# A's small softmax in smaller pieces, and the first stacked loads two per slot, in a kernel of two attentions

## The chip, the core and the metric

The kernel runs on one core of a Trainium2 chip. The metric is the device time of one execution in microseconds, as the median of several runs. A core has a matrix engine (PE, whose weight loads are shown apart as PEld), a vector engine (DVE), a scalar engine (ACT), a general engine (POOL) and a queue that starts DMAs (SP); ACT and POOL can start DMAs too. Each engine takes its instructions strictly in the order in which the program wrote them, and an instruction that waits holds up all behind it on its engine.

## What is computed

Two attentions over 2048 positions with 32 heads of 18 columns, each with its own input, its own projection and its own output matrix; the results stand side by side. A looks, from each position, at eight positions: itself and seven earlier ones, two apart. B looks at all positions.

```python
S, D, H, Dh, W, dil = 2048, 576, 32, 18, 8, 2
# A: q, k, v = heads of x @ wqkv
idx = arange(S)[:, None] - arange(W)[None, :] * dil      # masked where negative
logits = einsum("bhsd,bhswd->bhsw", q, k[idx]) * Dh ** -0.5
a = einsum("bhsw,bhswd->bhsd", softmax(logits), v[idx]) @ wo
# B: q, k, v = heads of x @ wqkv
scores = einsum("bhqd,bhkd->bhqk", q, k) * Dh ** -0.5
b = einsum("bhqk,bhkd->bhqd", softmax(scores), v) @ wo
out = concatenate([a, b], axis=-1)
```

## The kernel before

**Projections (up to about 415 us).** Inputs and weights are split into a high and a low part (L413, L414), and PE multiplies the parts (L303, L366). The products of B's queries and keys leave PSUM through ACT (L504, L505) and POOL (L506) and are stored by SP (L511) in a DRAM buffer `dqk`, those of A in `da` (L694, L695). The later part of this stage runs in *slots*: `stream` puts one product after the other on PE, and after each calls `slot()`, which takes one list of functions off `todo`. `at(n, f)` puts a function n slots on.

**Stacked queries and keys.** For four heads at a time (a *group* g, eight of them) queries and keys are read back from `dqk` in the layout that PE wants: `stack_loads(g)` returns twelve loads of 288 KB (L142, L143). For g = 0, 1 and 2 POOL issues them, in the slots of the projections. `second_rows` (L620) plans those of g = 1: it runs in a slot, and from there each load gets a slot of its own, from the fifth on.

**Steps.** After that there are 512 steps: eight groups times four *blocks* of 512 queries times sixteen key tiles. The blocks are numbered n = 0 to 31. Each step has four scores on PE (L271), four exponentials on ACT (L279), the product with the values of an earlier step's exponentials (L744), and, for later blocks, pieces of the row maxima: matmuls (L160) into a ring of three PSUM banks, each reduced by DVE (L168). PE can't refill a bank until DVE has reduced it. A block's maxima become a negative row that is loaded into the stacked queries (`place`, L193), so the first score of a block waits for these loads. Most steps open with the first part of a maximum and score behind it; where `ahead` (L1313) is true, the first score goes first. Before, it is true at a block's first step for n < 6 and n >= 24, unless the step is named in `MADE`.

**A beside it.** A's positions are worked on in eight pieces of 256, j = 0 to 7 (`local`, L902), on POOL and DVE while the steps run. `AT[j]` is the step at which j begins, and `plan` puts every part at a fixed step behind it; `due()` runs, at the end of each step, what is planned for it, so a DVE operation of A stands in DVE's queue behind the reductions of that step. `SOON[j]` moves the softmax of some j forward by one step (j = 4, 5, 6) or three (j = 0). The parts, in their order:

- `match` (L923): nine products of queries and keys on POOL, the last followed by L932, which writes the logits `lg`
- `most` (L945): the maximum over the eight logits, on DVE (L943, tile `am`), in two pieces of 32 columns, at steps 32 and 33 of j
- `lower` (L948, POOL), `exponents` (L951, ACT)
- `total` (L954): the sum, on DVE (L943, tile `as`): two pieces of 32 for j = 0, 2, 5, one of 64 for the others
- `inverses` (L957): two reciprocals on DVE (L959)
- `share` (L961): logits times reciprocals, on POOL (L962)
- `weighted` (L964): nine products with the values on POOL (L968 to L971), then `upper`, `rest`, `put` and `get`, which bring the result through DRAM to PE
- `sums_of_a`: the output product of A (L1260), for the most part in `together` (L1242), which takes two steps in one with the 27 matmuls of such a product beside them: a *pair* of steps, called a paired stretch below. `MADE` names the steps at whose end such a product becomes ready.

`match` of j + 1 begins on POOL soon after `weighted` of j.

Of the kernel before, what the change touches and what calls it, by code (L numbers as in the profile page):

```python
# [11 lines left out]
ALU = mybir.AluOpType  # L12
# [17 lines left out]
SUB = AB // 4  # L30
# [14 lines left out]
MADE = ((96, 101, 112, 128), (144, 160, 176, 192), (208, 212, 224, 240), (256, 266, 272, 288),  # L45
        (307, 320, 336, 352), (368, 376, 384, 400), (417, 432, 440, 448), (474, 476, 478, 480))
# [15 lines left out]
def two_attentions(ctx: ExitStack, tc, xa, wa, woa, xb, wb, wob, out):  # L62
# [45 lines left out]
    step = 0  # L108
# [8 lines left out]
    def due():  # L117
        for f in agenda.pop(step, []):
            f()
# [254 lines left out]
    def do_all(fs):  # L374
        for f in fs:
            f()
# [6 lines left out]
    with (tc.tile_pool(name="x", bufs=1, side="right") as xp,  # L383
# [103 lines left out]
        if True:  # L487
# [47 lines left out]
            ahead = deque()  # L535
# [29 lines left out]
            def at(n, *fs):  # L565

                while len(todo) <= n:
                    todo.append([])
                todo[n].extend(fs)
# [24 lines left out]
            def store_values(h, v2):  # L594
                for i, v in enumerate(v2):
                    load(dv[4 * h + 2 * i : 4 * h + 2 * i + 2].rearrange("g p t c -> p g (t c)"),
                         v.rearrange("p g t h d -> p g (t h d)"))
# [22 lines left out]
            def second_rows():  # L620

                store_values(1, v2)
                kept.close()
                stack1 = ctx.enter_context(tc.tile_pool(name="stack1", bufs=1, reuse_waits="tile"))
                make_set(stack1, 1)
                do_all(ones_loads(1))
                zeros = xp.tile([128, 512], F32, name="ohi", bufs=4)
                nc.gpsimd.memset(zeros[:108, : 16 * HALO], 0.0)
                load(rows(da[0], ((HALO + S) * 16, 108), (HALO + S, 16), (1, HALO)), zeros[:108, : 16 * HALO])
                for i, f in enumerate(stack_loads(1, issue=nc.gpsimd.dma_start)):  # L630
                    at(5 + i, f)
                load_v(0)

            wa_room = ExitStack()
# [48 lines left out]
            for k in range(2, 14):  # L683
                n = 46 if k == 2 else 36 + 4 * k
# [34 lines left out]
            for c, b in order:  # L719
                n = min(128, 3 * D - 128 * c)  # L720
                work_list.append(((b % 2, ws[c][0], xas[b][0], slice(0, n), every),
                                  lambda ps, n=n: ps[:n], lambda ps, c=c, b=b, n=n: leave_a(c, b, n, ps)))
# [12 lines left out]
        step = 0  # L735
# [166 lines left out]
    def local(j):  # L902
# [31 lines left out]
                    for w in range(1, W):  # L934
                        nc.gpsimd.memset(lg[:32, w, : DIL * w], MASKED)

        def over_window(op, name, n, parts=2):

            if n == 0:
                st[name] = work.tile([128, SUB], F32, name=name, bufs=1)  # L940
            some = SUB // parts
            cols = slice(some * n, some * n + some)
            nc.vector.tensor_reduce(st[name][:, cols], st["lg"][:, :, cols].rearrange("p w n -> p n w"), axis=AX.X, op=op)  # L943

        def most(n):  # L945
            over_window(ALU.max, "am", n)

        def lower():  # L948
            nc.gpsimd.tensor_sub(st["lg"], st["lg"], ap(st["am"], (0, W), (1, SUB)))
# [2 lines left out]
            nc.scalar.activation(st["lg"], st["lg"], AF.Exp, scale=SCALE)  # L952

        def total(n):  # L954
            over_window(ALU.add, "as", n, len(sums[0]))

        def inverses(n):  # L957
            half = st["as"][:, SUB // 2 * n : SUB // 2 * n + SUB // 2]
# [5 lines left out]
        def weighted(c):  # L964
            if c == 0:
                st["o"] = work.tile([128, DH, SUB], F32, name="ao", bufs=1)
            at = wide()
            nc.gpsimd.tensor_mul(at, ap(st["lg"], (0, 2), (SUB, W), (1, SUB)), window(st["v"], c))  # L968
            nc.gpsimd.tensor_add(at[:, :, :4], at[:, :, :4], at[:, :, 4:])  # L969
            nc.gpsimd.tensor_add(at[:, :, :2], at[:, :, :2], at[:, :, 2:4])  # L970
            nc.gpsimd.tensor_add(st["o"][:, 2 * c : 2 * c + 2], at[:, :, 0], at[:, :, 1])  # L971
# [10 lines left out]
        def put(i):  # L982
            load(rows(dao[j, i, 0, 0], (DH * SUB, 128), (1, DH * SUB)),
                 ap(st["parts"][i].bitcast(F32), (1, DH * SUB)))
# [24 lines left out]
        def sums_of_a(h, n, alone=True):  # L1009
# [7 lines left out]
            if not alone:  # L1017
# [4 lines left out]


        soon = SOON[j]
        sums = ((36, 37) if j in (0, 2, 5) else (36,), (38, 39))
        late = soon % 3
        pieces = [(33, lower), (35, exponents), (39, share), (60 + late, upper), (61 + late, rest), (64 + late, lambda: put(0)), (66 + late, lambda: put(1))]

        pieces[:0] = [(at, lambda f=f, n=n: f(n)) for f, ats in ((most, (32, 33)), (total, sums[0]),
                                                                (inverses, sums[1])) for n, at in enumerate(ats)]  # L1030
        for c in range(DH // 2):
            pieces.append((39 + 5 * c // 2 + late, lambda c=c: weighted(c)))
        pieces = [(at - soon, f) for at, f in pieces]
        pieces += [(5 + 5 * c // 2, lambda c=c: match(c)) for c in range(DH // 2)]

# [60 lines left out]
    sums = {}  # L1096
# [141 lines left out]
    rest = NG * NB * PIECES * 2 - early  # L1238

    total = early + rest  # L1240
# [47 lines left out]
    while step < ALL:  # L1288
        n, kt = divmod(step, NT)
        g, b = divmod(n, NB)  # L1290
        es = [None] * 4

        if inside and inside[0] in for_two and kt and len(ready) == 1 and total - sum(given) >= 8 and step + 4 < ALL:
            new = together(*inside.pop(0)(False))
            assert not leaving
            due()
            step += 1
            weigh(*ready, new[0])
            ready[:] = new[1:]
            due()  # L1300
            step += 1
            continue

        while leaving:
            leaving.pop()()

        whole = total - sum(given) > 1
        parts = (bool(begun) or total - sum(given) > 3) and step not in copied

        ps = bank() if inside and whole else None  # L1310


        ahead = kt == 0 and (n < 6 or n >= 24) and step not in sum(MADE, ())  # L1313
        part = [parts_of_maximum()] if parts and not ahead else []
        for h in (0, 2, 1, 3):

            if inside and h == 3:
                inside.pop(0)()
            es[h] = score(g, b, kt, h, between=(lambda: part.append(parts_of_maximum())) if parts and ahead and h == 0 else None)
            if h == 0 and whole:  # L1320
                maximum(1, ps)()
            if h == 1 and parts:
                part[0]()
            if h == 3 and whole:
                maximum(0)()
        if sum(given) == total and not begun:
            settle()
        for fs in (behind_scores, outside):
            while fs:
                fs.pop(0)()  # L1330

        paired = paired or kt % 2 == 0 and sum(given) == total and not begun
        for _ in range(1 if paired and step < ALL - 2 else len(waiting)):
            if waiting:
                waiting.pop(0)()
        if ready and (kt % 2 == 0 or not paired):
            weigh(ready.pop(0))
        ready.append((g, b, kt, es))
        if paired and kt % 2:
            weigh(*ready)  # L1340
            ready.clear()
        due()

        if len(waiting) > (0 if not paired else 2 if kt % 2 else len(waiting)):
            waiting.pop(0)()
        step += 1
# [24 lines left out]
```

## Time and profile before

| | |
|---|---|
| median of three runs | 1596.72 us (1595.77 to 1596.78) |
| the profiled execution | 1597.76 us, span 1596.0 us |
| mean granted clock of PE in it | 0.999 |
| PE busy | 1583.2 us (99%) |
| DVE busy | 1367.7 us (86%) |
| ACT busy | 1216.6 us (76%) |
| POOL busy | 964.6 us (60%) |

Engine shares are means over the span. In the order of time, a row has its start and its duration in us, the engine, the line, the operation with what it writes and reads, how many equal instructions are merged in it, and in brackets how long the engine had been idle before it and what ended that. In groups of instructions, the numbers behind the bar are the busy time in us, the mean duration of one in ns, and the idle time before them. Windows give the busy time of every engine in a stretch, with the number of instructions in brackets, and then the granted clock, the DMA share and GB/s. A busy PE is not PE at its peak: matmuls on the two halves of the rows overlap, and the rows don't show by how much.

### The profile page before, as it was taken

What the parts mean: (1) busy time and instruction counts of PE and PEld (TensorE: products, weight loads), DVE (VectorE), ACT (ScalarE), POOL (GpSimd) and SP (SyncE); (2) the same over time, 40 slices, a digit from 0 to 9 for tenths busy, and PEclk for the clock granted to TensorE, in tenths of its full rate; (3) what the DMA queues carried; (4) which work ended last, traced back from release to release, by engine and by line L of the source; (5) the groups of instructions that cost most, each with busy time, mean ns of one, the idle gap of its engine ahead of it and who ended that gap; (6) DMA issues with size and microseconds to landing.
All of it is one profiled execution on the core that took longest, in us unless ns stands there. A gap on an engine that the chain in (4) does not pass through costs nothing.

```text
span 1596.0 us, 34951 instructions
## 1 busy us (share of the span) xinstructions
PE 1583.2 (99%) x13276; PEld 969.1 (61%) x13276; DVE 1367.7 (86%) x2294; ACT 1216.6 (76%) x2438; POOL 964.6 (60%) x798
## 2 busy tenths in 40 slices
PE   9999999999999999999999999999999999999998
PEld 7999889999644445444445445445444444545676
DVE  5199899999999999999989999999999999998622
ACT  6423441211599999999999999999999999998655
POOL 2405742211166996896797897797798699791000
PEclk9999999999999999999999999999999999999999
DMA  8937954622312262245326324522721332154311
GB/s 254 232 124 201 255 178 124 164 90 81 74 34 71 64 143 63 70 118 123 74 67 138 90 79 114 123 67 54 148 89 50 90 94 56 51 166 139 129 60 63
DMA packets 188024, 175.65 MB, mean 110 GB/s; under 512 B 119416, under 2 KB 133240, under 8 KB 186128
## 3 DMA queue, kind: packets, MB, share of 16 engines
q1 hardware_dynamic: 182992, 161.88, 37.0%
q0 software_dynamic: 4032, 10.63, 3.2%
q8 instruction: 104, 1.70, 0.5%
q10 hardware_dynamic: 832, 0.92, 0.2%
q14 instruction: 64, 0.52, 0.1%
HBM read 98.77 MB, written 73.47 MB: 108 GB/s over the span
## 4 chain that ended last, share of the span: by engine, by line
PE 92%; DVE 5%; DMA 1%; ACT 1%; POOL 1%; issue 0%; SPq 0%; POOLq 0%; DVEq 0%; ACTq 0%
PE po L744 29%; PE bank L271 18%; PE bank L160 17%; PE bank L366 15%; PE bank L303 5%; PE bank L1260 4%; PE bank L1133 4%; DVE mx L168 4%; POOL xlo L414 1%; ACT e L279 0%; DMA dqk<-olo 0%; DVE am L943 0%; DMA first<-xb 0%; DMA more<-xa 0%; DMA dqk<-ohi 0%
## 5 line engine op out<-in xcount | busy, mean ns | idle before, releaser
L168 DVE TENSOR_REDUCE mx<-bank 128x2 f32<-128x512 f32 x2048 | 1279.7, 684 | 121.6 <-PE bank L160 91.1
L279 ACT ACTIVATE e<-bank 128x512 f32<-128x512 f32 x2048 | 1048.3, 605 | 61.2 <-PE bank L271 55.3
L160 PE MATMUL bank<-ks,qs 54*128 54x512 f32 (+1 forms) x2466 | 789.0, 381 | 4.2 <-DVE mx L168 3.4
L160 PEld LDWEIGHTS bank<-ks,qs 54*128 54x128 f32 x2466 | 404.1, 184 | 390.2 <-DVE mx L168 343.8
L271 PE MATMUL bank<-qs,ks 56*128 56x512 f32 x2048 | 592.2, 425 | 0.1
L744 PE MATMUL po<-e,v 128*19 128x512 f32 x4096 | 531.3, 598 | 0.0
L271 PEld LDWEIGHTS bank<-qs,ks 56*128 56x128 f32 x2048 | 308.3, 184 | 25.5 <-ACT e L279 18.8
L925 POOL TENSOR_TENSOR pr<-aq,akv 128x1024 f32<-128x1024 f32 x72 | 158.4, 2201 | 15.9 <-PE po L744 13.1
L968 POOL TENSOR_TENSOR pr<-lg,akv 128x1024 f32<-128x1024 f32 x72 | 158.3, 2199 | 0.5
L744 PEld LDWEIGHTS po<-e,v 128*19 128x19 f32 x4096 | 73.8, 97 | 138.2 <-issue 132.8
L929 POOL TENSOR_TENSOR pr<-pr 128x1024 f32<-128x1024 f32 x64 | 152.5, 2383 | 5.0
L694 ACT ACTIVATE ohi<-bank 128x512 f32<-128x512 f32 (+1 forms) x56 | 30.4, 595 | 148.9 <-issue 114.0
L366 PE MATMUL bank<-xhi,ahi 64*128 64x512 f32 (+1 forms) x448 | 115.4, 387 | 0.0
L366 PE MATMUL bank<-xhi,alo 64*128 64x512 f32 (+1 forms) x448 | 111.3, 387 | 0.0
L366 PE MATMUL bank<-xlo,ahi 64*128 64x512 f32 (+1 forms) x448 | 108.3, 388 | 0.1
L1260 PE MATMUL bank<-wohi,at 64*128 64x288 f32 x480 | 104.1, 305 | 0.0
L969 POOL TENSOR_TENSOR pr<-pr 128x512 f32<-128x512 f32 x72 | 92.5, 1285 | 5.6
L1260 PEld LDWEIGHTS bank<-wohi,at 64*128 64x128 f32 x480 | 74.9, 184 | 27.6 <-ACT e L279 23.8
L414 POOL TENSOR_TENSOR alo<-raw,ahi 128x512 fp32r<-128x512 f32 (+1 forms) x14 | 17.6, 1254 | 121.1 <-ACT ahi L413 96.3
L506 POOL TENSOR_TENSOR olo<-olo,ohi 128x512 fp32r<-128x512 f32 x36 | 46.1, 1294 | 65.7 <-ACT ohi L505 55.6
L1260 PE MATMUL bank<-wolo,at 64*128 64x288 f32 x240 | 70.2, 293 | 0.0
L366 PEld LDWEIGHTS bank<-xhi,ahi 64*128 64x128 f32 (+1 forms) x448 | 65.0, 182 | 2.6
(200 smaller groups left out, 1797.3 us busy)
## 6 DMA issues: line engine op xcount, KB each, us to landing
do<-n SPq DMA_DIRECT2D x30, 512.0 KB
da<-ohi SPq DMA_DIRECT2D x52, 256.0 KB
akv<-da SPq DMA_DIRECT2D x64, 175.5 KB
out<-y SPq DMA_DIRECT2D x32, 288.0 KB
qs<-dqk SPq DMA_DIRECT2D x30, 288.0 KB
ks<-dqk SPq DMA_DIRECT2D x30, 288.0 KB
at<-dao SPq DMA_DIRECT2D x60, 128.0 KB
rec<-drec SPq DMA_DIRECT2D x29, 256.0 KB
```

The costliest lines, as they stand in the source:

```text
L160: return nc.tensor.matmul(ps if part is None else ps[:, 256 * r : 256 * r + 256], qs[at, b, p, 128 * t : 128 * t + 128], ks[at, p, 512 * k ...
L168: nc.vector.tensor_reduce(at, ps.rearrange("q (s n) -> q s n", s=2), axis=AX.X, op=ALU.max)
L271: nc.tensor.matmul(ps, ks[at, p, 128 * kt : 128 * kt + 128], qs[at, b, p], start=True, stop=True)
L279: nc.scalar.activation(e, ps, AF.Exp, scale=SCALE)
L303: nc.tensor.matmul(ps, a, b, start=c == i == 0, stop=c == 4 and i == 1)
L366: nc.tensor.matmul(ps, a, b, start=start, stop=stop)
L744: nc.tensor.matmul(po[32 * i : 32 * i + 19], vs[g][:, kt, 19 * i : 19 * i + 19], es[i], start=kt == 0, stop=kt == NT - 1)
L925: nc.gpsimd.tensor_mul(pr, ap(st["q"][:, 2 * c], (SUB, 2), (0, W), (1, SUB)), window(st["k"], c))
L929: nc.gpsimd.tensor_add(st["pr"], st["pr"], pr)
L968: nc.gpsimd.tensor_mul(at, ap(st["lg"], (0, 2), (SUB, W), (1, SUB)), window(st["v"], c))
L969: nc.gpsimd.tensor_add(at[:, :, :4], at[:, :, :4], at[:, :, 4:])
L1260: return nc.tensor.matmul(ps, a, b, start=r == k == 0, stop=r == 1 and k == len(both[1]) - 1)
```

## The change

A's maxima are taken in four pieces of 16 columns, or in three of 24, 20 and 20 (j = 3, 4, 5), one per step, the last where the last one was. The sums are taken in four pieces of 16 (j = 0, 2, 5) or three of 32, 16 and 16 (the others), from the step where they began before. The reciprocals and the share move back by one step, or by two for j = 0, 2, 5, and the first of the products with the values is not planned ahead of the share. The twelve stacked loads of g = 1 go two per slot from the fourth slot on. `ahead` is true from block 23 on, also where the step is in `MADE`.

```diff
                 for i, f in enumerate(stack_loads(1, issue=nc.gpsimd.dma_start)):
-                    at(5 + i, f)
+                    at(4 + i // 2, f)
                 load_v(0)
...
-        def over_window(op, name, n, parts=2):
-
-            if n == 0:
+        def over_window(op, name, a, z):
+
+            if a == 0:
                 st[name] = work.tile([128, SUB], F32, name=name, bufs=1)
-            some = SUB // parts
-            cols = slice(some * n, some * n + some)
+            cols = slice(a, z)
             nc.vector.tensor_reduce(st[name][:, cols], st["lg"][:, :, cols].rearrange("p w n -> p n w"), axis=AX.X, op=op)
 
         def most(n):
-            over_window(ALU.max, "am", n)
+            over_window(ALU.max, "am", *highest[n])
...
         def total(n):
-            over_window(ALU.add, "as", n, len(sums[0]))
+            over_window(ALU.add, "as", *summed[n])
...
         soon = SOON[j]
-        sums = ((36, 37) if j in (0, 2, 5) else (36,), (38, 39))
+        alone = j in (0, 2, 5)
+        summed = [(16 * n, 16 * n + 16) for n in range(4)] if alone else [(0, 32), (32, 48), (48, 64)]
+        highest = [(0, 24), (24, 44), (44, 64)] if j in (3, 4, 5) else [(16 * n, 16 * n + 16) for n in range(4)]
         late = soon % 3
-        pieces = [(33, lower), (35, exponents), (39, share), (60 + late, upper), (61 + late, rest), (64 + late, lambda: put(0)), (66 + late, lambda: put(1))]
-
-        pieces[:0] = [(at, lambda f=f, n=n: f(n)) for f, ats in ((most, (32, 33)), (total, sums[0]),
-                                                                (inverses, sums[1])) for n, at in enumerate(ats)]
+        pieces = [(33, lower), (35, exponents), (40 + alone, share), (60 + late, upper), (61 + late, rest), (64 + late, lambda: put(0)), (66 + late, lambda: put(1))]
+
+        pieces[:0] = [(at, lambda f=f, n=n: f(n)) for f, ats in ((most, range(34 - len(highest), 34)),
+                                                                (total, range(36, 36 + len(summed))),
+                                                                (inverses, (39 + alone, 40 + alone))) for n, at in enumerate(ats)]
         for c in range(DH // 2):
-            pieces.append((39 + 5 * c // 2 + late, lambda c=c: weighted(c)))
+            pieces.append((max(39 + 5 * c // 2 + late, 40 + alone), lambda c=c: weighted(c)))
         pieces = [(at - soon, f) for at, f in pieces]
...
-        ahead = kt == 0 and (n < 6 or n >= 24) and step not in sum(MADE, ())
+        ahead = kt == 0 and (n < 6 or n >= 23)
```

## The prediction

> **What bounds the kernel now.** I read the page first, then the order of time on PE's weight loads, then DVE's groups, then POOL over long windows.
>
> ```profile
> span 1596.0 us, 34951 instructions
> ...
> PE 1583.2 (99%) x13276; PEld 969.1 (61%) x13276; DVE 1367.7 (86%) x2294; ACT 1216.6 (76%) x2438; POOL 964.6 (60%) x798
> ```
>
> PE is never idle for long, so the end moves only by what makes PE wait or run slower. From 415 us on, the work goes in steps, and each opens with a weight load for a maximum (L160). In the order of time on PEld:
>
> ```profile
> 502.94 0.18 PEld L160 LDWEIGHTS bank<-ks,qs 54*128 54x128 f32 x1 [1.10 <-DVE mx L168]
> 505.25 0.18 PEld L160 LDWEIGHTS bank<-ks,qs 54*128 54x128 f32 x1 [1.15 <-DVE mx L168]
> ...
> 1209.82 0.18 PEld L160 LDWEIGHTS bank<-ks,qs 54*128 54x128 f32 x1 [0.85 <-DVE mx L168]
> 1211.86 0.18 PEld L160 LDWEIGHTS bank<-ks,qs 54*128 54x128 f32 x1 [0.85 <-DVE mx L168]
> ```
>
> An undisturbed step takes 1211.86 - 1209.82 = 2.04 us, and its 0.85 is only the time in which PE still multiplies by the values. The step from 502.94 to 505.25 takes 2.31: DVE had one of A's maxima in its queue, and PE's next bank was 0.27 late. DVE's groups by shape give the sizes:
>
> ```profile
> L943 DVE TENSOR_REDUCE am<-lg 128x32 f32<-128x256 f32 x16 | 9.7, 605 | 0.0
> L959 DVE RECIPROCAL as<-as 128x32 f32<-128x32 f32 x16 | 5.4, 341 | 0.0
> L943 DVE TENSOR_REDUCE as<-lg 128x64 f32<-128x512 f32 x5 | 5.3, 1064 | 1.9 <-ACT lg L952 1.9
> ```
>
> So 0.605 us of extra DVE work costs a step 0.27: about 0.34 us per step is free. From 0.605 for 32 columns and 1.064 for 64, I estimate 0.14 + 0.0143 per column: 0.37 for 16 columns, 0.43 for 20, 0.49 for 24.
>
> **The change, part by part.**
>
> **1. Smaller pieces.** Before: 16 maxima of 32 columns, 6 sums of 32, 5 of 64. After: 29 maxima (five j with four of 16, three with 24, 20 and 20) and 27 sums. Some of either fall in paired steps, where PE has A's output products to do and DVE has room. Of the old ones I count 14 maxima and about 6 sums in plain steps, at 0.27 each about 5.4 us. The new ones exceed the free 0.34 by 0.03 (16 columns) to 0.15 (24); some 40 in plain steps come to about 2.1, two or three of them beside another small DVE operation in the same step. Net -3.3, between -5.4 (all free) and 0 (the price follows total DVE time, which rises).
>
> **2. What moves with them.** The share (L962, POOL) waits for the second reciprocal, and that is now due one step later (j = 1, 3, 4, 6, 7) or two (j = 0, 2, 5). At the other end, the first maximum is due one step earlier (j = 3, 4, 5) or two (the rest). Between the share of one j and the first maximum of the next lies one unbroken run of POOL work: nine products by values, then nine matches, ending in L932, which the maximum reads. Windows over two of these runs (columns: length; then busy time of PE, PEld, DVE, ACT, POOL):
>
> ```profile
> 1127.20:1225.40 98.20, 98.11 (x807) 47.01 (x809) 89.23 (x149) 94.21 (x188) 94.71 (x69) 1.00 0.41 103
> 1248.10:1349.50 101.40, 101.38 (x827) 47.90 (x827) 92.24 (x154) 96.92 (x193) 97.72 (x73) 1.00 0.30 78
> ```
>
> POOL is busy 94.71 of 98.20 us with 69 instructions, 0.05 us between two: nothing in it can shrink, so a share that starts later ends L932 as much later. How long L932 had been done when the first maximum started, in the order of time (j = 1, 3, 4, 5, 6, 7):
>
> ```profile
> 618.75 1.29 POOL L932 TENSOR_TENSOR lg<-pr 128x512 f32<-128x512 f32 x1
> 627.00 0.60 DVE L943 TENSOR_REDUCE am<-lg 128x32 f32<-128x256 f32 x1
> 865.69 1.28 POOL L932 TENSOR_TENSOR lg<-pr 128x512 f32<-128x512 f32 x1
> 869.38 0.62 DVE L943 TENSOR_REDUCE am<-lg 128x32 f32<-128x256 f32 x1
> 983.56 1.28 POOL L932 TENSOR_TENSOR lg<-pr 128x512 f32<-128x512 f32 x1
> 988.80 0.60 DVE L943 TENSOR_REDUCE am<-lg 128x32 f32<-128x256 f32 x1
> 1105.44 1.29 POOL L932 TENSOR_TENSOR lg<-pr 128x512 f32<-128x512 f32 x1
> 1109.23 0.60 DVE L943 TENSOR_REDUCE am<-lg 128x32 f32<-128x256 f32 x1
> 1224.16 1.29 POOL L932 TENSOR_TENSOR lg<-pr 128x512 f32<-128x512 f32 x1
> 1230.82 0.60 DVE L943 TENSOR_REDUCE am<-lg 128x32 f32<-128x256 f32 x1
> 1348.28 1.28 POOL L932 TENSOR_TENSOR lg<-pr 128x512 f32<-128x512 f32 x1
> 1353.84 0.61 DVE L943 TENSOR_REDUCE am<-lg 128x32 f32<-128x256 f32 x1
> ```
>
> The room (start of L943 less end of L932) is 6.96, 2.41, 3.96, 2.50, 5.37 and 4.28. Taken from it are the steps of the share before and of the earlier maximum, 2.04 each:
> - j = 4: 3.96 - 4.1 = -0.1; j = 5: 2.50 - 4.1 = -1.6, and its share's reciprocal now falls behind the head of a paired stretch, 0.25 more: -1.85.
> - j = 6: 5.37 - 8.1 = -2.7; j = 7: 4.28 - 6.1 = -1.8.
> - j = 3: both its pieces stay behind the same paired stretch, so nothing is lost there, but j = 2's reciprocals ran early, in a paired stretch, and now run in a plain step: its share moves from 766.44 to the head of the step at 770.46, plus 0.4 to the place in the step (head at 1353.40, j = 7's maximum at 1353.84), plus 0.34 for the reciprocal, some 4.9 later. 2.41 - 4.9 = -2.5.
> - j = 1: 6.96 less four steps is below zero too, but its first two pieces stand behind a paired stretch with room; I take 0. j = 2 loses three steps and I take 0; j = 0 has no run before it.
>
> ```profile
> 766.44 1.29 POOL L962 TENSOR_TENSOR lg<-lg,as 128x512 f32<-128x512 f32 x1 [12.69 <-DVE as L959]
> 770.46 0.18 PEld L160 LDWEIGHTS bank<-ks,qs 54*128 54x128 f32 x1 [0.85 <-DVE mx L168]
> ...
> 1353.40 0.18 PEld L160 LDWEIGHTS bank<-ks,qs 54*128 54x128 f32 x1 [0.85 <-DVE mx L168]
> ...
> 870.72 1.89 DVE L168 TENSOR_REDUCE mx<-bank 128x2 f32<-128x512 f32 x3 [0.71 <-PE bank L160]
> ```
>
> DVE takes its queue in order. Behind a maximum that waits for L932 stand the reductions that free PE's three banks, so PE stops as soon as they are full, and the step is longer by the wait, plus the piece, less 0.34. j = 4: 0.2. j = 5: 1.85 + 0.49 - 0.34 = 2.0. j = 6: 2.7 + 0.37 - 0.34 = 2.7. j = 7: 1.8 + 0.03 = 1.8. At j = 3 both pieces (0.8) follow the late L932 at 871.9, and the next reduction starts at 872.7, not at 870.72: 2.0. Sum +8.7, between 0 (should POOL win the steps back) and 11 (j = 1 and 2 stop as well).
>
> **3. The clock behind such a stop.** The trace has one stop of this length, in the projections: on PE, on ACT and in windows (the last columns: granted clock, DMA share, GB/s).
>
> ```profile
> 175.16 0.59 PE L366 MATMUL bank<-xhi,whi 64*128 64x512 f32 x2 [1.70 <-ACT olo L504]
> ...
> 172.84 0.63 ACT L413 ACTIVATE xhi<-raw 128x512 fp32r<-128x512 f32 x1 [10.43 <-DMA raw<-xa]
> ...
> 170.00:174.00 4.00, 3.45 (x30) 3.02 (x27) 4.00 (x8) 1.12 (x3) 0.45 (x1) 1.00 1.01 276
> 174.00:178.00 4.00, 2.84 (x14) 2.28 (x16) 1.18 (x3) 3.89 (x7) 3.90 (x5) 0.68 0.95 301
> 178.00:182.00 4.00, 4.00 (x34) 3.27 (x34) 3.40 (x6) 2.91 (x6) 3.93 (x4) 0.90 1.01 331
> 182.00:186.00 4.00, 4.00 (x38) 3.48 (x36) 3.95 (x7) 0.63 (x1) 3.90 (x7) 1.00 1.03 306
> ```
>
> PE was idle 0.55 + 1.16 = 1.7 us, the clock was 0.68 and 0.90 in the next two windows, and of 3 x 38 matmuls 36 were missing, or 3.8 us: 2.1 beyond the idle time. Four stops of 1.8 to 2.7 us are as long or longer. I take 1.1 for each, half the price, because while PE is slow DVE gets ahead and the pieces that follow are free: +4.4, between 0 and 8.4.
> The Trainium skill, "TensorE: Matmul & The Clock Gate", Part 1, says that the clock falls back after an idle window of about 3.4 us. By that rule no stop here is long enough, and this part would be 0; the 1.70 us gap above speaks against it.
>
> **4. Block heads.** `ahead` now holds at every block's first step from block 23 on. Blocks 23, 24, 25, 27 and 28 change; the first step of 30 lies in a pair and doesn't use it. On PEld, block 23's first step, and block 29's, which had the new order already:
>
> ```profile
> 1213.89 0.18 PEld L160 LDWEIGHTS bank<-ks,qs 54*128 54x128 f32 x1 [0.85 <-DVE mx L168]
> 1214.26 0.18 PEld L271 LDWEIGHTS bank<-qs,ks 56*128 56x128 f32 x1 [0.19 <-issue]
> 1216.25 0.18 PEld L1260 LDWEIGHTS bank<-wohi,at 64*128 64x128 f32 x1 [0.85 <-ACT e L279]
> ...
> 1427.81 0.18 PEld L271 LDWEIGHTS bank<-qs,ks 56*128 56x128 f32 x1 [0.85 <-ACT e L279]
> 1429.97 0.18 PEld L271 LDWEIGHTS bank<-qs,ks 56*128 56x128 f32 x1 [0.85 <-ACT e L279]
> ```
>
> With the maximum first the step took 2.36, with the score first 2.16: 0.2 won at each of four heads (block 24 shows no such wait; an ordinary 2.04 there becomes 2.16, 0.1 lost). -0.7, between -1.6 (all of the 0.32 over 2.04, at five) and +0.6 (0.12 lost at five).
>
> **5. The first stacked loads.** Twelve loads of 288 KB on POOL's queue, issued between
>
> ```profile
> 134.08 0.69 POOL L143 DMA_DIRECT2D qs<-dqk  x1
> ...
> 188.47 0.60 POOL L142 DMA_DIRECT2D ks<-dqk  x1
> ```
>
> now go in six slots instead of twelve and end near 153. Their first use is some 18 slots later, so they are late for nobody. They leave the time in which ACT waits 10.43 us for an x row (row at 172.84), the cause of the 3.8 us above. But SP's queue is held by its own landings, and eight loads in ten microseconds may delay the rows that are fetched then, and with them the very one ACT waits for. POOL's issue time (0.6 to 0.7 each) only changes place. All of the stop gone is -3.8; the x row 3 us later is +3. I take -2, nearer the first: the last loads now stand well ahead of 160, and a wait 1 us shorter already saves part of the clock.
>
> **Sum.** -3.3 + 8.7 + 4.4 - 0.7 - 2.0 = +7.1 on the profiled execution's 1597.76, or 1604.9. That execution is 1.04 above the median of the runs, so I forecast 1604 as median (0.2%, or 3.2 us, is about what a measurement of this kernel can tell).
>
> **The rivals.**
> - *Faster: POOL doesn't hold DVE.* If the runs of POOL had slack that the windows hide, parts 2 and 3 fall away: -3.3 - 0.7 - 2.0 = -6.0, 1591. For it: POOL waited 12.69 us before the share at 766.44, so it is not short of time over a whole j. Against it: that wait lies ahead of the share, not behind it, and between share and L932 there are 3.5 us in all. It decides when the room stays above zero at j = 3, 5, 6 and 7, that is when L932 comes 2 us earlier than I work out. 0.16.
> - *The stops come, the clock holds.* 1604.9 - 4.4 less the 1.04: 1599.5. For it: one instance is thin, and there 0.55 us of idling lay just ahead of the stop. Against it: the stops forecast are longer than that one's 1.70 us. 0.2. This is what the Trainium skill's page above would make of it.
> - *The loads collide.* Part 5 at +3 or more, the rest as forecast: 1609. For it: a DMA share of 0.95 to 1.03 in the windows of part 3. 0.12.
> - *As forecast*, 1601 to 1608: 0.48; the last 0.04 is a change that comes to nothing.
>
> **How the numbers follow.** Slower is the forecast (0.48), the colliding loads (0.12) and a part of the second rival (0.08): 0.68. Same is the rest of that rival and the last case: 0.16. Faster: 0.16. The range leaves out the first rival and the far end of the third: 1595 to 1610; the forecast's own is 1601 to 1608.
>
> **What would show it.** The changed kernel's waits name DVE am L943 behind POOL lg L932, some 9 us in four or five waits, longest at j = 6; L932 ends later than its first maximum could start; the clock falls below 1.0 just behind them; L943 has 56 instructions. If there is no such wait and POOL's runs are as long as before, part 2 is wrong. Part 4 shows as L271 opening blocks 23 to 28; part 5 as a wait of ACT for raw<-xa well under 10.43 us and a clock of 1.0 between 174 and 182.

## The result and the profile after

The changed kernel takes 1605.91 us (median, 1604.71 to 1610.28), the kernel before, run beside it, 1596.75 us (1595.42 to 1598.99). The ratio is 1.0061, with a 95% interval from 1.0048 to 1.0075: slower by 0.6%, and the interval leaves out 1. The forecast was 1604, with 1601 to 1608 as its own range. The profiled execution took 1605.57 us. Of all the runs reported below, one of *loads behind the stretch* took 2596.74 us at a granted clock of 0.712 and is left out of that kernel's ratio.

The page of the changed kernel: the span, the busy times, and, from further down, the shares of the chain that ended last.

```profile
span 1603.8 us, 34982 instructions
...
PE 1584.1 (99%) x13276; PEld 972.9 (61%) x13276; DVE 1367.9 (85%) x2323; ACT 1217.7 (76%) x2438; POOL 966.3 (60%) x798
...
PE 60%; POOL 27%; DVE 5%; DMA 3%; issue 3%; ACT 1%; SPq 1%; POOLq 0%; DVEq 0%; ACTq 0%
```

PE is as busy as before and has as many matmuls; the shares of busy time tell nothing of the 7.8 us by which the span grew. The chain does: 27% of it now runs over POOL, where it was 1% before: at each of the new stops it turns back along POOL's run of work.

Where the time went in the order of the span is told by the first and the last of the 512 steps. Their first scores on PE, of the kernel before:

```profile
414.68 0.39 PE L271 MATMUL bank<-qs,ks 56*128 56x512 f32 x1
...
1581.05 0.79 PE L271 MATMUL bank<-qs,ks 56*128 56x512 f32 x4
```

and of the changed kernel:

```profile
416.66 0.39 PE L271 MATMUL bank<-qs,ks 56*128 56x512 f32 x1
...
1588.87 0.78 PE L271 MATMUL bank<-qs,ks 56*128 56x512 f32 x4
```

The steps begin 1.98 us later (the projections lost it) and take 1172.21 us instead of 1166.37, or 5.84 more. What follows the last step takes as long as before.

**In the steps.** The waits of the changed kernel (engine, line waited for: us in total, times, longest):

```profile
DVE am L942 <- POOL lg L932: 7.5, 4, 2.5
...
PE bank L160 <- DVE mx L168: 8.3, 8, 2.0
```

The first row is new; of the second the kernel before had 3.4 us, none longer than 0.4. In the order of time, at j = 3, 5, 6 and 7: the end of POOL's run (L932), the first maximum behind it, and the next weight of a maximum that PE can load (L942 is L943 of before).

```profile
871.39 1.29 POOL L932 TENSOR_TENSOR lg<-pr 128x512 f32<-128x512 f32 x1
872.72 0.81 DVE L942 TENSOR_REDUCE am<-lg 128x24 f32<-128x192 f32 x2 [2.50 <-POOL lg L932]
874.78 0.38 PE L160 MATMUL bank<-ks,qs 54*128 54x256 f32 x1 [1.89 <-DVE mx L168]
...
1110.28 1.28 POOL L932 TENSOR_TENSOR lg<-pr 128x512 f32<-128x512 f32 x1
1111.60 0.49 DVE L942 TENSOR_REDUCE am<-lg 128x24 f32<-128x192 f32 x1 [1.30 <-POOL lg L932]
1113.34 0.38 PE L160 MATMUL bank<-ks,qs 54*128 54x256 f32 x1 [1.43 <-DVE mx L168]
...
1231.14 1.28 POOL L932 TENSOR_TENSOR lg<-pr 128x512 f32<-128x512 f32 x1
1232.45 0.37 DVE L942 TENSOR_REDUCE am<-lg 128x16 f32<-128x128 f32 x1 [1.80 <-POOL lg L932]
1234.08 0.38 PE L160 MATMUL bank<-ks,qs 54*128 54x256 f32 x1 [2.02 <-DVE mx L168]
...
1357.11 1.28 POOL L932 TENSOR_TENSOR lg<-pr 128x512 f32<-128x512 f32 x1
1358.42 0.37 DVE L942 TENSOR_REDUCE am<-lg 128x16 f32<-128x128 f32 x1 [1.94 <-POOL lg L932]
1360.04 0.38 PE L160 MATMUL bank<-ks,qs 54*128 54x256 f32 x1 [1.96 <-DVE mx L168]
```

Each time the maximum starts within 0.05 us of the end of L932, and PE follows with a stop of 1.4 to 2.0 us. Step by step against the trace of before, those four steps are 1.96, 1.55, 2.08 and 2.04 us longer, and the one at j = 4 is 0.25 longer.

What the clock did behind the stops shows in windows laid on the grid on which the clock's records begin (start and end, length, busy time of PE, PEld, DVE, ACT, POOL, then granted clock, DMA share, GB/s):

```profile
870.57:873.98 3.41, 2.32 (x20) 0.84 (x16) 1.26 (x3) 2.06 (x4) 2.04 (x2) 1.00 0.55 127
873.98:877.40 3.42, 2.62 (x20) 1.32 (x22) 3.42 (x8) 2.06 (x4) 1.27 (x1) 1.00 0.58 198
...
1232.38:1235.80 3.42, 1.72 (x16) 0.84 (x16) 3.35 (x8) 1.38 (x4) 3.28 (x5) 1.00 0.01 2
1235.80:1239.21 3.41, 3.41 (x20) 1.51 (x16) 3.12 (x7) 2.94 (x6) 0.29 (x2) 0.50 0.00 0
...
1358.68:1362.09 3.41, 2.05 (x16) 0.84 (x16) 3.41 (x8) 1.51 (x4) 3.25 (x5) 1.00 0.10 20
1362.09:1365.51 3.42, 3.42 (x32) 1.76 (x32) 3.42 (x7) 3.34 (x8) 1.42 (x2) 1.00 0.28 104
```

Only the stop at j = 6 is followed by a window at half clock; the two steps in that window are 0.20 and 1.03 us longer. The stops at j = 3 and 7 are as long, and the clock stays at 1.00 (the row at 1362.09 for j = 7).

**At the block heads.** On PEld, block 23's first step now opens with the score:

```profile
1217.73 0.18 PEld L271 LDWEIGHTS bank<-qs,ks 56*128 56x128 f32 x1 [0.85 <-ACT e L279]
...
1219.89 0.18 PEld L1262 LDWEIGHTS bank<-wohi,at 64*128 64x128 f32 x1 [0.85 <-ACT e L279]
```

It takes 2.16 us, 2.36 before.

**In the projections.** SP's loads of block maxima (`qs<-mh`, `qs<-mt`) and of x rows (`raw<-xa`), in the order of time, of the kernel before:

```profile
149.16 3.25 SPq L197 DMA_DIRECT2D qs<-mh  x4
152.75 8.03 SPq L197 DMA_DIRECT2D qs<-mt  x4
166.17 1.77 SPq L407 DMA_DIRECT2D raw<-xa  x3
```

and of the changed kernel, with ACT's wait for the row, PE's stop and the windows behind it:

```profile
149.85 6.73 SPq L197 DMA_DIRECT2D qs<-mh  x4
158.67 7.64 SPq L197 DMA_DIRECT2D qs<-mt  x4
171.64 1.77 SPq L407 DMA_DIRECT2D raw<-xa  x3
...
174.80 0.63 ACT L413 ACTIVATE xhi<-raw 128x512 fp32r<-128x512 f32 x1 [8.36 <-DMA raw<-xa]
177.12 0.50 PE L366 MATMUL bank<-xhi,whi 64*128 64x512 f32 x2 [3.34 <-ACT olo L504]
...
174.00:178.00 4.00, 0.88 (x6) 0.79 (x8) 0.42 (x2) 3.14 (x6) 2.49 (x3) 0.96 0.99 270
178.00:182.00 4.00, 4.00 (x24) 3.17 (x24) 2.68 (x5) 2.63 (x5) 3.82 (x4) 0.62 1.02 272
```

POOL's loads are over earlier, at 153, but SP now needs 6.73 us instead of 3.25 for four small loads, and reaches the x rows 5.5 us later. ACT's wait became shorter (8.36, not 10.43) and ended later (174.80, not 172.84): where a wait begins late, its length says little. PE stands for 3.34 us instead of 1.70.

### The profile page after: what moved, and what is told of

It is laid out like the page before. It is cut to its first block, busy times and chain, and to the rows that moved or that the text cites. A ratio compares the mean times of both kernels' runs of the same rounds, so it can differ in the third digit from the quotient of the medians.

```text
span 1603.8 us, 34982 instructions
## 1 busy us (share of the span) xinstructions
PE 1584.1 (99%) x13276; PEld 972.9 (61%) x13276; DVE 1367.9 (85%) x2323; ACT 1217.7 (76%) x2438; POOL 966.3 (60%) x798
## 4 chain that ended last, share of the span: by engine, by line
PE 60%; POOL 27%; DVE 5%; DMA 3%; issue 3%; ACT 1%; SPq 1%; POOLq 0%; DVEq 0%; ACTq 0%
PE po L744 16%; PE bank L366 13%; PE bank L160 10%; PE bank L271 10%; POOL pr L925 6%; POOL pr L929 5%; POOL pr L967 5%; PE bank L303 5%; DVE mx L168 4%; PE bank L1135 4%; POOL pr L968 3%; PE bank L1262 2%; POOL pr L969 2%; DMA raw<-xa 1%; POOL ao L970 1%
## 5 line engine op out<-in xcount | busy, mean ns | idle before, releaser
L103 POOL CAST mh<-mt 128x32 fp32r<-128x32 f32 x32 | 6.8, 212 | 116.3 <-DVE mt L185 116.3
```

## The experiments

The theory after the result has three parts: POOL's run between the share and L932 is rigid, so that every step that a share loses is lost at the next maximum; such a stop costs its length, and now and then a window at half clock; the stacked loads cost what they hold up in SP's queue. In this table stand the medians, the ratio to the kernel before with its 95% interval (taken over the runs, so it is not exactly the quotient of two medians), and, from one profiled execution each, the start of the first step and the time from there to the start of the last (the kernel before: 414.68 and 1166.37).

| kernel | median us | ratio | first step at | 511 steps |
|---|---|---|---|---|
| the change | 1605.91 | 1.0061 (1.0048 to 1.0075) | 416.66 | 1172.21 |
| softmax alone | 1603.49 | 1.0045 (1.0030 to 1.0060) | 414.79 | 1172.36 |
| small early maxima alone | 1595.94 | 0.9997 (0.9987 to 1.0006) | 413.48 | 1164.67 |
| small sums, later share alone | 1598.52 | 1.0016 (1.0006 to 1.0026) | 413.05 | 1168.17 |
| loads alone | 1600.66 | 1.0025 (1.0014 to 1.0037) | 417.55 | 1166.39 |
| heads alone | 1596.14 | 0.9993 (0.9984 to 1.0002) | 413.57 | 1165.94 |
| share two steps later still | 1636.16 | 1.0244 (1.0225 to 1.0262) | 413.38 | 1205.70 |
| small pieces, share kept | 1596.19 | 0.9999 (0.9990 to 1.0008) | 414.87 | 1166.30 |
| loads late | 1598.08 | 1.0007 (0.9998 to 1.0016) | 414.68 | 1166.43 |
| loads behind the stretch | 1596.10 | 0.9995 (0.9985 to 1.0004) | 412.94 | 1167.21 |
| softmax in its room | 1593.99 | 0.9984 (0.9975 to 0.9993) | 412.89 | 1163.69 |
| both | 1593.50 | 0.9977 (0.9967 to 0.9986) | 412.36 | 1163.59 |

### The change in its parts

**Softmax alone**: all of the softmax's edits, the loads and `ahead` as before.

> The changed softmax alone, stacked loads and block heads as before. Room theory (a stop is the lateness of POOL's logits at the first maximum, room before less share shift less the earlier maximum): DVE waits for L932 at j = 3, 4, 5, 6, 7 for 0.2 to 2.6 us, in all 7 to 9 us; time +6.5 us over before, 5.3 if the clock falls nowhere, up to 10 if it falls at each of four stops. Rival (the added time is that of more DVE instructions): no wait for L932, and the added time spread over the steps with pieces.

The steps took 5.99 us more, and the median lies 6.8 us above that of the kernel before in the same comparison (1596.66). The waits name the same cause, and PE's stop at j = 7 the place:

```profile
DVE am L942 <- POOL lg L932: 6.8, 4, 2.4
...
1356.40 0.38 PE L160 MATMUL bank<-ks,qs 54*128 54x256 f32 x1 [1.82 <-DVE mx L168]
...
1356.00:1360.00 4.00, 3.60 (x18) 1.48 (x20) 3.40 (x7) 2.06 (x4) 3.38 (x3) 0.58 0.18 57
```

This time the clock fell behind j = 7 and not behind j = 6: of the stops it is one, and not always the same one, that is paid for twice.

**Small early maxima alone**: the sums, reciprocals and share stay where they were.

```diff
+        summed = [(0, 32), (32, 64)] if alone else [(0, 64)]
+        highest = [(0, 24), (24, 44), (44, 64)] if j in (3, 4, 5) else [(16 * n, 16 * n + 16) for n in range(4)]
...
-        pieces[:0] = [(at, lambda f=f, n=n: f(n)) for f, ats in ((most, (32, 33)), (total, sums[0]),
+        pieces[:0] = [(at, lambda f=f, n=n: f(n)) for f, ats in ((most, range(34 - len(highest), 34)),
```

> Only the maxima in smaller pieces, one or two steps earlier; sums, reciprocals and share as before. Room theory: the room before less one or two steps stays above zero at every j (smallest 0.2 at j = 7 and 0.5 at j = 5), so DVE never waits for L932 and the smaller pieces win: -1.5 to -2.5 us. Rival (the earlier maxima alone collide with POOL): stops at j = 5, 6, 7 of 2 us, +3 to +5 us.

No maximum waits; the group of 16 columns, in the groups by shape (behind the last bar stands the idle time before them), has no idle time, where the change has 3.7 us of it:

```profile
L942 DVE TENSOR_REDUCE am<-lg 128x16 f32<-128x128 f32 x20 | 7.4, 372 | 0.0
```

The steps are 1.70 us shorter in the profiled execution, but what follows the last step took 0.9 us longer in it; the median is 0.7 lower, which can't be told from no change. An earlier maximum by itself does no harm: there is room for it.

**Small sums and the later share alone**: two maxima of 32 as before.

```diff
+        highest = [(0, 32), (32, 64)]
...
+        pieces = [(33, lower), (35, exponents), (40 + alone, share), (60 + late, upper), (61 + late, rest), (64 + late, lambda: put(0)), (66 + late, lambda: put(1))]
```

> Only sums in smaller pieces, reciprocals and share one or two steps later; two maxima of 32 columns where they were. Room theory: only j = 3 runs out of room (2.41 less 4.9), a stop of 1.8 us there; j = 5 keeps 0.2, the others more than 1; smaller sums win 1: +0.5 to +1.5 us (up to 2.5 if the clock falls at j = 3). Rival (the later share alone makes the stops): waits at j = 3, 5, 6, 7, +4 to +6 us.

One stop, at j = 3, of 1.61 us, and the steps 1.80 us longer. The later share by itself harms only where the room was smallest. Both together do more than the sum of both: +5.99 in the steps against +1.80 - 1.70. What they share is the room, and each alone stays inside it except at j = 3. That is what a threshold looks like.

**Loads alone.**

```diff
-                    at(5 + i, f)
+                    at(4 + i // 2, f)
```

> Only the stacked loads two per slot from the fourth on. My forecast was -2. From the changed kernel's profile (first step 1.98 us later): ACT's wait ends 2 us later than before, because SP's place loads wait for landings longer and the x row is issued 5 us later: +1.5 to +2 us. Rival (that difference is run to run noise): 0.

The gain of 2 us that the prediction had is refuted: 1600.66 against 1596.66. The steps are untouched (1166.39), and all of the loss lies ahead of them. The order of time and the windows:

```profile
174.86 0.63 ACT L413 ACTIVATE xhi<-raw 128x512 fp32r<-128x512 f32 x1 [9.11 <-DMA raw<-xa]
...
174.00:178.00 4.00, 0.82 (x4) 0.73 (x6) 0.04 (x1) 3.07 (x6) 2.43 (x2) 0.70 1.04 274
178.00:182.00 4.00, 4.00 (x20) 3.11 (x20) 2.20 (x4) 3.26 (x6) 3.84 (x4) 0.50 1.04 324
```

Here the clock was low for two windows; in the change it was one; a first step that starts 0.9 us later still fits that.

**Heads alone.**

```diff
-        ahead = kt == 0 and (n < 6 or n >= 24) and step not in sum(MADE, ())
+        ahead = kt == 0 and (n < 6 or n >= 23)
```

> Only the block heads: first score first at every block from 23 on. By the forecast's part 4 and the changed kernel's steps: -0.2 at blocks 23, 25, 27, 28, +0.2 at 24, together -0.6 us; within 0.3 us of no change would mean that the steps around give it back.

Blocks 23, 25 and 28 win 0.2 each over two steps, 24 loses 0.2, 27 wins 0.1, and block 29's head, which isn't edited, loses 0.35: the loads of its maxima came too late for it (the last section). The steps are 0.43 us shorter; the median can't be told from no change.

### How rigid POOL's run is

**Share two steps later still**: the change's softmax and heads, with share and reciprocals at two more steps.

```diff
-        pieces = [(33, lower), (35, exponents), (40 + alone, share), ...
+        pieces = [(33, lower), (35, exponents), (42 + alone, share), ...
```

> The changed softmax and block heads with reciprocals and share two steps later still, stacked loads as before: the suspected wait made longer by 4.1 us at every j from 1 on. Room theory: stops at all seven, about 3.7 (j = 1), 2.5, 6.1, 4.3, 5.7, 6.2, 6.1 us, some 34 us over before. Clock: if a stop of 4 us and more always drops it, at least five falls and 1 to 2 us more for each, +40 to +45 in all; if a fall is as rare as in the changed kernel (one in five stops), one or two and +35 to +37. Rival to the room theory (the share's place doesn't matter): time as with the changed softmax alone.

The steps took 1205.70 us, 39.3 more than before. At j = 2 to 7 the first maximum now waits for L932, and its step is longer by 2.01, 3.93, 4.32, 4.56, 5.94 and 6.08 us; the clock fell behind the last five of these. The waits, and a window behind the stop at j = 7:

```profile
DVE am L942 <- POOL lg L932: 26.5, 6, 6.0
...
1389.20:1392.60 3.40, 3.40 (x17) 1.28 (x16) 2.17 (x5) 2.07 (x4) 2.16 (x3) 0.50 0.24 79
```

From the change to this, the stops at j = 4, 6 and 7 grew by 4.07, 3.86 and 4.04 us for two steps of 2.04: there POOL gives back nothing. At j = 3 and 5 they grew by 1.97 and 3.01. At j = 3 POOL's run was 2.1 us shorter (98.48 instead of 100.56), because two operations of B that stood in it (`o<-o,rec`, `n<-o`) ran ahead of the late share. At j = 5 the run was as long as in the change, but a step ahead of the maximum (1095.72) had become 1.83 us longer, in which PE waits for `at<-dao`, so the maximum came later too. Beyond such single operations, this refutes the prediction's first rival, in which POOL's runs have the slack to take a share's delay.

A seventh stop, 3.48 us at 594, is of another kind: 30 us ahead of the end of j = 1's L932, PE waits for stacked keys.

```profile
596.77 0.47 PE L160 MATMUL bank<-ks,qs 54*128 54x512 f32 x1 [2.25 <-DMA ks<-dqk]
```

The loads of these keys stand in SP's queue behind `put`, which stores A's result, and SP waits 13.8 us there for POOL (9.8 before, 12.4 in the change, where it made no stop yet): a late share holds up SP as well. The clock fell behind this stop too. It and the step behind it made the steps 3.9 us later, so that j = 1's maximum found its logits ready 1.48 us ahead, where a stop of 3.7 had been expected.

**Small pieces, share kept**: the reciprocals in one piece of 64 instead of two of 32, so that three sums fit and the share stays.

```diff
+        summed = [(0, 24), (24, 44), (44, 64)]
+        highest = [(0, 24), (24, 44), (44, 64)] if j in (3, 4, 5, 7) else [(16 * n, 16 * n + 16) for n in range(4)]
...
-            nc.vector.reciprocal(half, half)
+            nc.vector.reciprocal(st["as"], st["as"])
```

> Smaller maxima where room is left (three pieces also at j = 7), three sums of 24, 20 and 20, one reciprocal of 64 columns at the share's old step so that the share doesn't move, the new block heads without block 24, stacked loads as before. Room theory: no wait for L932, -3 to -4 us against before. Rival (smaller pieces only add DVE time): 0 to +2.

The expected gain did not come: 1596.19, no change. No maximum waits for L932, but a reciprocal of 64 columns takes 0.54 us in one step where 0.34 are free, sums of 20 and 24 take 0.43 and 0.48, and block 29's head lost 0.79. Steps with such a piece, where there was none before, became 0.1 to 0.3 us longer, and together with that head this took back what the other small pieces won.

### The loads

**Loads late**: from the 22nd slot on, two per slot.

```diff
+                    at(22 + i // 2, f)
```

> Only the stacked loads, two per slot, but from the 22nd slot on, behind the x rows and still ahead of their first use. If they are what makes the x rows late: ACT's wait of 10.43 us shrinks, PE's 1.70 us stop and the clock's fall behind it go, -2.5 to -3.8 us. If SP's own queue and not the stacked loads makes the x row late: within 0.5 us of before. If they come too late for their first use: a new wait of PE for qs or ks near 260 us.

The first half is as expected, and the second takes it back. In the order of time:

```profile
149.02 2.35 SPq L197 DMA_DIRECT2D qs<-mh  x4
...
165.95 0.63 ACT L413 ACTIVATE xhi<-raw 128x512 fp32r<-128x512 f32 x1 [3.43 <-DMA raw<-xa]
...
222.01 0.50 PE L366 MATMUL bank<-xlo,ahi 64*128 64x512 f32 x1 [1.25 <-POOL xlo L414]
...
225.65 0.50 PE L366 MATMUL bank<-xlo,ahi 64*128 64x512 f32 x2 [1.21 <-POOL xlo L414]
```

ACT's wait fell to 3.43 us and PE no longer stops near 175. But now POOL issues the loads between 204 and 228, when it has x rows to split, and PE waits for those instead. The first step starts at 414.68, exactly as before.

**Loads behind the stretch**: from the 26th slot on, three per slot.

```diff
+                    at(26 + i // 3, f)
```

> The kernel before with the twelve stacked loads of g = 1 moved behind the projections' busiest stretch: three per slot from the 26th slot on, not one per slot from the fifth. Theory (what these loads cost is their landing time inside the stretch in which x rows are fetched, whichever slots they take): ACT's wait of 10.43 us for an x row shrinks by half or more, PE's 1.70 us gap near 175 and the half clock behind it are gone, and POOL issues the loads where no x rows are left to split, so the waits of PE for xlo that loads_late had at 222 and 226 us don't come: the first step starts 2 to 3.5 us earlier, 1593.5 to 1595.5. Rival (the loads are now late for their first use at about 252 us): PE waits there for qs or ks, and the time is that of the kernel before or above, 1597 to 1600.

```profile
223.12 0.50 PE L366 MATMUL bank<-xlo,ahi 64*128 64x512 f32 x2 [1.08 <-POOL xlo L414]
```

Two stops became one, and the first step starts at 412.94. The median is no better than before (0.9995, 0.9985 to 1.0004), so the expected 2 to 3.5 us did not come. Two things took them. First, the 1.74 us won at the first step are against one profiled execution of the kernel before, and this moment varies: the seven other kernels of the table that leave the loads alone, and so have the same projections, reach the first step between 412.89 and 414.87 us. Second, the steps are 0.84 us longer, 0.76 of it at block 29's head.

### What fits the room

**Softmax in its room**: small pieces only where the room covers them, so that the share moves by two steps for j = 0 and 5, by one for j = 7, and not at all otherwise; j = 6 keeps two maxima of 32; the score goes first at two heads more, 23 and 25.

```diff
+        alone = {0: 2, 5: 2, 7: 1}.get(j, 0)
+        summed = ([(0, 32), (32, 48), (48, 64)] if j == 7 else [(16 * n, 16 * n + 16) for n in range(4)] if alone
+                  else [(0, 32), (32, 64)] if j == 2 else [(0, 64)])
+        highest = [(0, 24), (24, 44), (44, 64)] if j in (3, 4, 5) else [(0, 32), (32, 64)] if j == 6 else [(16 * n, 16 * n + 16) for n in range(4)]
...
+        ahead = kt == 0 and (n < 6 or n in (23, 25, 26, 29, 31))
```

> Small pieces only where POOL's run has room for them: maxima in four of 16 (j = 0, 1, 2, 7), three of 24, 20 and 20 (j = 3, 4, 5), two of 32 at j = 6; small sums with a share one step later at j = 7, two later at j = 0 and 5, and the old sums and shares for the others; the score first at block 23 and at 25, 26, 29 and 31, as before at 24 and 30. Loads as before. Theory (a share costs only what exceeds the room up to the next maximum): no wait for L932 at any j, no fall of the clock in the steps, steps 2 to 3 us shorter, 1594 to 1595. Rival (the gain of small pieces is lost again to pieces that fall together and to later heads, as with share_kept): 1596 to 1597.

**Both**: this and the loads behind the stretch.

> softmax_in_room and loads_behind together. Theory: their gains lie in different stages and add: 1590 to 1592.5, faster than both kernels. Rival: one of the two comes to nothing, 1594 to 1597.

Softmax in its room takes 1593.99 us, a ratio of 0.9984 (0.9975 to 0.9993): fewer of the small pieces, and only where the room covers them, are a gain. No maximum waits for L932, and the steps are 2.68 us shorter, as expected; at j = 7 the room is used up to the last (the maximum starts 0.03 us after the end of L932). PE's gap in the projections is still there, this time without a fall of the clock:

```profile
174.95 0.50 PE L366 MATMUL bank<-xhi,whi 64*128 64x512 f32 x2 [1.54 <-ACT olo L504]
...
174.00:178.00 4.00, 3.05 (x26) 2.55 (x28) 2.24 (x4) 3.89 (x8) 3.90 (x5) 1.00 0.94 292
```

Both together take 1593.50 us, 0.9977 (0.9967 to 0.9986), faster than both kernels. They were expected at 1590 to 1592.5; the loads added 0.5 us at most, which can't be told from nothing by the medians.

## Why the prediction was right, point by point

The time was right within 2 us and the sign was right for the reason given, but two of the five terms were wrong, in opposite directions. In the profiled executions the span grew by 7.8 us, against a sum of +7.1.

- **Part 1, smaller pieces (-3.3).** About -2.6: what is left of the 5.84 us in the steps once the stops (7.88), the fall of the clock behind them (1.23) and the heads (-0.7) are taken out. Softmax in its room, without any stop, won 2.68 us, some 0.4 of it at the heads. The mechanism held: steps of 2.3 us that carried 0.605 us of extra DVE work came down to about 2.08 with 0.37. Some of it was lost where a piece meets another small operation of DVE in one step: those that began at 646.29, 1003.75 and 1374.36, with L178 beside the piece, became 0.17 to 0.24 us longer.
- **Part 2, what moves with them (+8.7).** Right, place by place: 1.96, 0.25, 1.55, 2.08 and 2.04 us at j = 3 to 7, or 7.88, where 2.0, 0.2, 2.0, 2.7 and 1.8 were forecast, and nothing at j = 1 and 2. Two runs that halve the edit, and one that delays the share by two steps more, support it: a stop comes where delay and earlier maximum together exceed the room, and at j = 4, 6 and 7 it grew by the full 2.04 us a step from there. But "nothing in it can shrink" was too strong. Operations of POOL that don't depend on the share ran ahead of it when it came late. At j = 6 that was one of B's (`n<-o,n`, 1.29 us), and the run was 0.9 us shorter, hence the miss there. (At j = 5 the 0.25 us added for the paired stretch didn't come: against the steps, j = 4's share was 2.05 us later.) At j = 1 the nothing that was taken was luck: the splitting of an output weight stood behind the share (at 517.12) before, and ahead of it (at 523.13) in the change:

```profile
524.07 1.43 POOL L104 TENSOR_TENSOR wolo<-y,wohi 128x576 fp32r<-128x576 f32 x1
...
515.42 1.43 POOL L104 TENSOR_TENSOR wolo<-y,wohi 128x576 fp32r<-128x576 f32 x1
```

With its other half (L103) that took 2.05 us out of the run, 100.87 us instead of 102.92. 1.11 us of room were left; had the splitting stayed in the run, I estimate from these numbers a stop of some 0.9 us.

- **Part 3, the clock (+4.4).** Mis-sized: 1.2 us. A fall costs about what was assumed (1.23 here, 1.41 in softmax alone), but only one of four stops of 1.4 to 2.0 us had one. The step that failed is "four stops of 1.8 to 2.7 us are as long or longer": length is not what decides (below). The prediction had one instance and charged it to all. Nor did the rule of the Trainium skill that it set against that instance hold ("TensorE: Matmul & The Clock Gate", Part 1: the clock falls after an idle window of about 3.4 us): by that no stop here would have a fall.
- **Part 4, the heads (-0.7).** About as forecast: -0.22 or -0.23 each at 23, 25 and 28, from 2.36 to 2.16 us for the first step of block 23, +0.2 at 24, and -0.1 to -0.3 at 27, where a smaller maximum falls in the same steps; together -0.6 to -0.8. Unforeseen was that block 29's head can lose again what those before it won.
- **Part 5, the stacked loads (-2.0).** Wrong in sign: +2.0 in the profiled execution, and +4.0 in the medians when made alone. The prediction named the mechanism against it (SP's queue is held by its own landings) and gave that a rival at 0.12, but let the end of POOL's issues at 153 outweigh it. What counts is when the bytes land. SP's loads of maxima wait in its queue for earlier DMAs to land, and these waits grew (for `dqk<-ohi` from 0.9 to 4.4 us between 140 and 176). The landing of POOL's own `ks` loads took longer too: in the issues of DMAs (operation, times, size, median us from issue to landing), before

```profile
ks<-dqk POOLq DMA_DIRECT2D x18, 288.0 KB, 7.1
```

and with the change

```profile
ks<-dqk POOLq DMA_DIRECT2D x18, 288.0 KB, 10.6
```

The Trainium skill, "DMA: Bandwidth & Descriptors", section "Issuing engines are not separate DMA queues", has the rule that speaks for this: whichever engine issues a DMA, it runs on the same sixteen DMA engines. The trace agrees: with twelve loads of POOL moved out of the stretch, SP's four loads take 2.35 us, with them spread 3.25, with them packed 6.73.

The base of part 5 was off as well. The 3.8 us that it put on the stop near 175 came from one execution, in which the clock had fallen. In the seven kernels with the same projections the windows there held 0.7 to 1.7 us of idling and the clock did not fall, and the first step started up to 1.8 us earlier (412.89 in softmax in its room) or 0.2 later (414.87 in small pieces, share kept). So there was less to win than the prediction thought; that this execution stood 1.04 us above the median was a hint of it.

Parts 3 and 5 missed by -3.2 and +4.0 and nearly cancelled; the forecast's 1604 owes part of its closeness to that.

## What to carry to other kernels

When work on one engine is cut into smaller pieces, ask first what each piece delays: between two engines that pass work back and forth there is a fixed room, edits that push from its two ends draw on the same room, and each may be harmless alone. Cut only where the room covers it, and count for every piece what it takes beyond what its step has free. Read also what else stands in the queues behind the work that moves, and what may run ahead of it. For DMAs, packing the issues closer moves no bytes sooner; look at what stands in other queues behind the same landings, and read when a wait ends, not how long it is.

## What the runs showed of the hardware

**The clock falls by what one window holds, not by the length of a stop.** In each trace the stretches at half clock begin on a grid of 3.413 us (in the change at 177.66 and 1235.80, 310 periods apart). Taken over the windows of this grid, PE's idle time before a fall from full clock was 1.69 (the change, j = 6: the length less the busy time in the row at 1232.38, before rounding), 1.70 (before, near 175), 1.82 (softmax alone, j = 7), and 1.89 or more in the others. Windows at full clock with 1.66 (heads alone, near 175), 1.62 (share two steps later still, j = 2), 1.54 (the later share alone, j = 3), 1.37 (the change, j = 7) and less were followed by none. So the fall came at about half a window of idling, and a stop that a boundary of the grid cuts in two goes free: at j = 3 of the change, 1.09 us lie in one window and 0.80 in the next. As the grid runs free of the kernel, the same stop is charged in one execution and not in another. Once the clock is low, less is enough to keep it so: in share two steps later still it stayed at half for a second window after one with 0.82 us of idling.
The Trainium skill, "TensorE: Matmul & The Clock Gate", Part 1, describes a free-running window of about 3.4 us, and the grid agrees; that it takes a whole idle window the falls above contradict.

**A head that nobody touched can become late.** Block 29's first score came 0.35, 0.79 and 0.76 us later in heads alone, small pieces with the share kept and loads behind the stretch, and not in softmax in its room, though that reached it sooner than these three. What differs is SP: it was through with issuing that block's `qs<-mt` loads 1.04, 1.49 and 1.44 us after the start of the step ahead of the head, against 0.18 before, 0.38 in the change and 0.02 in softmax in its room. SP's waits there are for DMAs to land (4.5 us for `ks<-do` in small pieces with the share kept, 3.3 before; 2.2 for `y<-wob` in loads behind the stretch). Why these landed later stays open.
